# A fused attention and gMLP block: SyncE's transfers in program order during attention, placed by booked engine ends and landing times

## The chip, the cores and the metric

The kernel runs on one core of a Trainium2 chip. The metric is the device time of one execution in microseconds. TensorE (PE in the profile) does the matmuls, VectorE (DVE) and ScalarE (ACT) work on their results, GpSimd (POOL) helps, and SyncE (SP) issues nearly all DMA transfers.

## The reference

The input `x` is 2048 rows of 576. It is normalised, and two branches use the result: a banded attention with 32 heads of width 18, and a gated MLP whose gate mixes the rows with a 2048 x 2048 matrix. Cut to what matters:

```python
xn = layernorm(x)
# A: attention, each row sees itself and the 255 rows before it
q, k, v = split(xn @ wqkv)                      # 32 heads, Dh = 18
p = softmax(where(mask, q @ k.T * Dh**-0.5, -1e9))
s = (p @ v) @ wo
# B: gated MLP, Fh = 2304
z = gelu(xn @ w_in)
z1, z2 = z[..., :Fh], layernorm(z[..., Fh:])
g = w_sp @ z2 + b_sp[:, None]
out = x + s * silu((z1 * g) @ w_out)
```

## The kernel before

Values are kept to float32 by splitting an operand into a high and a low part and multiplying three times (`split`: the high part on ScalarE, the rest on VectorE). The program runs in stages: projections of q, k and v with z2 (up to 447 us), attention with the z1 projection (447 to 987 us), the projection by `wo`, the large product with `w_sp` (`acc`, line 1080), and the last product with `w_out`.

The change lies in the attention stage. It has sixteen **units** of four heads and half of the rows (`UNITS`, eight for the first half, eight for the second). A unit does this:

- Its q and k are loaded from DRAM into **slots** (`att`), five buffers of one pair of heads each, by `load_pair` (lines 343 to 354, sixteen transfers for two pairs). Slots 3 and 4 are cleared first (`clear`).
- **Row maxima** for the softmax are computed one unit ahead (`row_max`): 32 matmuls into `sp` (line 392, two PSUM buffers), a masked maximum on VectorE each (line 396), a transpose (line 402), two operations that make `mhl`, a store to `m_d` (line 410) and four reloads into rows of the slot (line 414), so that the maximum is subtracted inside the score matmul.
- **Scores**: matmuls into `tps` (line 513, two PSUM buffers) and an exponential on ScalarE into `pt` (line 517); then `pv` multiplies by the values `vg` into `ops` (line 537), and ScalarE copies the unit's output to `ou` (line 547).
- **Division** (`finish`): the row sums go from `ou` to `den` by DMA (line 586), VectorE takes the reciprocal (line 559), it is stored to `r_d` and read back, repeated over 32 rows, into `rp` (lines 561 and 564), VectorE multiplies in two halves (line 572), and four stores write `o_d` (line 581).

Between these short matmuls the planner puts the **z1** projection as filling: chunks of 14 matmuls of 512 columns (line 443), a copy `z1o` on ScalarE (line 446) and a store (line 448). The weights of a block of four chunks come by one load `z1raw` (line 421) and are split in six pieces (line 452). In the last unit five pieces of `wo` are loaded (line 715) and split too.

The order on TensorE, VectorE, GpSimd and ScalarE is the order in which this code is run: `tc.manual_schedule` covers them from line 724. The planner keeps a `clock` that every matmul moves on by its booked time (`spend`), the booked ends of ScalarE and VectorE (`busy`, `use`), and a list of jobs with a due time (`after`, run by `tick` once the clock has passed it). SyncE is not covered there: the order of its queue comes from the framework's own scheduler. A transfer is issued when the queue reaches it and its semaphores allow; eight semaphores take turns.

`due` spreads a unit's scores evenly over its span, and the row maxima of the next unit from its begin to the share `RM1` of the span; the first `EARLY` maxima of the unit after that begin at the share `RM2`. `WEIGHT` sets how many z1 matmuls each unit gets.

Of the kernel before, what the change touches and what calls it, by code (L numbers as in the profile page):

```python
# [9 lines left out]
F32 = mybir.dt.float32  # L10
# [6 lines left out]
P = 128  # L17
# [22 lines left out]
EARLY = 6  # L40
RM2 = 0.78
RM1 = 0.74
# [5 lines left out]
_SHARE = [18 + 0.4 * (i >= 8) for i in range(16)]  # L48
# [12 lines left out]
def kernel(  # L61
# [153 lines left out]
    with ExitStack() as early:  # L215
# [109 lines left out]
        with ExitStack() as ph:  # L325
# [3 lines left out]
            def clear(i):  # L329
                eng = (dve, pool)[i % 2]  # L330
                eng.memset(f32(slots[i][:, 0:2 * HS]), 0.0)
                eng.memset(f32(slots[i][:, 2 * HS:]), 1.0)
# [10 lines left out]
            def load_pair(p):  # L343
# [4 lines left out]
                for j in (2 * a, 2 * a + 1):  # L348
                    h, b = 4 * g + j, 64 * (j % 2)
                    q, k = f32(q_of(u, j)), f32(k_of(u, j))  # L350
                    sp.dma_start(q[b:b + 36, :], st_d[0, 0:36, h, q0:q0 + HS])
                    sp.dma_start(k[b:b + 18, :kn], st_d[1, 18:36, h, k0:k0 + kn])
                    sp.dma_start(q[b + 36:b + 56, :], st_d[0, 18:38, h, q0:q0 + HS])
                    sp.dma_start(k[b + 18:b + 54, :kn], st_d[1, 0:36, h, k0:k0 + kn])
# [25 lines left out]

            def row_max(u):
# [3 lines left out]
                for j in range(4):  # L385
                    for i in range(8):
                        qb = 8 * half + i
                        w = 384 if qb >= 2 else 256
# [20 lines left out]
                def put_max():  # L409
                    sp.dma_start(m_d[u], f32(m))  # L410
                    rows = m_d[u].rearrange("(n j i) q -> n j (i q)", n=2, j=4)
# [4 lines left out]
                after(500, put_max)  # L416
# [15 lines left out]
            def z1_matmuls():  # L432
                nxt = z1_first.pop()
                for f in range(FH // P):
# [3 lines left out]
                    for c in range(NC):  # L438
# [3 lines left out]
                        for n, (w, r) in enumerate(pl):  # L442
                            pe.matmul(ps, w, r, start=n == 0, stop=n == len(pl) - 1)  # L443
                            if n == len(pl) - 1:
                                zo = zw.tile([P, 512], F32, name="z1o", bufs=3)
                                act.activation(zo, ps, AF.Copy)
                                use("act", 620)
                                sp.dma_start(z1_d[f * P:(f + 1) * P, cs], zo)
                                if c == 0 and f + 1 < FH // P:
                                    nxt = load_z1(f + 1)  # L450
# [101 lines left out]
            def finish(u, ou):  # L552
# [5 lines left out]
                def put_inverse():  # L558
                    dve.reciprocal(den, den)
                    use("dve", 350)  # L560
                    sp.dma_start(r_d[u].rearrange("h (a b) -> (h a) b", b=HS // 32), den)
# [4 lines left out]
                def invert():  # L566
                    put_inverse()
                    get_inverse()
# [6 lines left out]
                def divide():  # L575
# [3 lines left out]
                    for i in range(4):  # L579
                        h = 4 * g + i  # L580
                        sp.dma_start(o_d[h * DH:(h + 1) * DH, cs], ou[32 * i:32 * i + DH, :])

                if u == NU - 1:
                    last.extend([lambda: sp.dma_start(den, ou[DH::32, :]), put_inverse, get_inverse, divide])
                else:
                    after(700, lambda: sp.dma_start(den, ou[DH::32, :]))
# [126 lines left out]
            def load_wo(k):  # L713
                raw = wors[k % 2]
# [509 lines left out]
```

## Time and profile before

| | |
|---|---|
| median of three timed runs | 1970.8 us (1968.49, 1970.8, 1975.66) |
| the profiled execution | 1975.21 us, its span 1973.5 us |
| TensorE's mean granted clock in it | 0.997 |
| matmuls of attention: z1, scores, row maxima (all units), ops | 1008, 576, 512, 1408 |
| a unit, from its first score to the next one's | 31.0 us (first half, 544.9 to 575.9 us), 33.7 us (second half, 770.5 to 804.2 us) |
| DMA in the profile | 375.58 MB, 190 GB/s in the mean |

In a row of the profile stand the line, the engine, the operation and the tiles it writes and reads; idle time ahead of an instruction is given with the instruction that ended it. `PEld` is the load of weights, which overlaps the matmuls. `SPq` is an instruction of SyncE's queue.

### The profile page before, as it was taken

What the parts mean: (1) busy time and instruction counts of PE and PEld (TensorE: products, weight loads), DVE (VectorE), ACT (ScalarE), POOL (GpSimd) and SP (SyncE); (2) the same over time, 40 slices, a digit from 0 to 9 for tenths busy, and PEclk for the clock granted to TensorE, in tenths of its full rate; (3) what the DMA queues carried; (4) which work ended last, traced back from release to release, by engine and by line L of the source; (5) the groups of instructions that cost most, each with busy time, mean ns of one, the idle gap of its engine ahead of it and who ended that gap; (6) DMA issues with size and microseconds to landing.
All of it is one profiled execution on the core that took longest, in us unless ns stands there. A gap on an engine that the chain in (4) does not pass through costs nothing.

```text
span 1973.5 us, 30747 instructions
## 1 busy us (share of the span) xinstructions
PE 1930.6 (98%) x11096; PEld 1650.5 (84%) x11096; DVE 1054.4 (53%) x2296; ACT 897.9 (45%) x1674; POOL 283.9 (14%) x360
## 2 busy tenths in 40 slices
PE   6999999999999999999899999999999999999998
PEld 5889999997777777777698887888888888899998
DVE  6511233266666666656125778656877567663222
ACT  4222322215555556655546675655554534442121
POOL 5000366202322223323200000000000000000000
PEclk9999999999999999999999999999999999999999
DMA  8656799424454656454476777776677555775441
GB/s 244 181 148 171 247 339 344 178 78 137 139 155 137 160 140 159 137 144 125 141 239 224 258 230 238 249 236 205 209 233 247 181 185 177 263 231 159 140 146 57
DMA packets 221368, 375.58 MB, mean 190 GB/s; under 512 B 43296, under 2 KB 118176, under 8 KB 221088
## 3 DMA queue, kind: packets, MB, share of 16 engines
q1 hardware_dynamic: 205856, 349.66, 57.2%
q10 hardware_dynamic: 15360, 23.97, 3.3%
q8 instruction: 87, 1.43, 0.3%
q14 instruction: 65, 0.53, 0.1%
HBM read 260.45 MB, written 112.83 MB: 189 GB/s over the span
## 4 chain that ended last, share of the span: by engine, by line
PE 85%; DMA 6%; DVE 4%; issue 2%; SPq 1%; ACT 1%; POOL 1%; DVEq 0%; ACTq 0%; POOLq 0%
PE acc L1080 31%; PE po L1151 11%; PE mm L443 10%; PE mm L667 8%; PE mm L296 5%; PE sp L392 5%; PE tps L513 4%; PE ops L537 4%; PE wops L845 3%; PE vps L463 3%; DMA att<-st_d 1%; DMA den<-ou 1%; DMA xr<-in_x_dram 1%; DMA a<-in_w_sp_dram 1%; DVE spl L112 0%
## 5 line engine op out<-in xcount | busy, mean ns | idle before, releaser
L1080 PE MATMUL acc<-spl,zh 128*128 128x512 f32 x1008 | 392.8, 390 | 1.4 <-DVE spl L112 1.2
L1080 PE MATMUL acc<-sph,zl 128*128 128x512 f32 x1008 | 392.2, 389 | 0.0
L1080 PE MATMUL acc<-sph,zh 128*128 128x512 f32 x1008 | 392.2, 389 | 0.0
L396 DVE CUSTOM_DVE_ANT_0 junk<-sp,band 128x384 bf16<-128x384 f32 (+1 forms) x512 | 269.1, 537 | 174.0 <-PE sp L392 167.9
L517 ACT ACTIVATE pt<-tps 128x384 f32<-128x384 f32 (+2 forms) x576 | 244.3, 437 | 190.3 <-PE tps L513 180.1
L443 PE MATMUL mm<-b,z1wh 128*128 128x512 f32 x648 | 236.3, 396 | 0.0
L1080 PEld LDWEIGHTS acc<-spl,zh 128*128 128x128 f32 x1008 | 189.2, 188 | 42.7 <-DVE spl L112 3.5
L112 DVE TENSOR_TENSOR spl<-spr,sph 128x1024 fp32r<-128x1024 f32 x168 | 205.2, 1221 | 32.7 <-ACT sph L111 30.2
L1080 PEld LDWEIGHTS acc<-sph,zh 128*128 128x128 f32 x1008 | 189.2, 188 | 39.2
L1080 PEld LDWEIGHTS acc<-sph,zl 128*128 128x128 f32 x1008 | 189.2, 188 | 39.1
L667 PE MATMUL mm<-z2wh,b 128*128 128x384 f32 x720 | 191.5, 335 | 2.1 <-ACT zt L677 2.1
L111 ACT ACTIVATE zh<-b 128x384 fp32r<-128x384 f32 x168 | 87.4, 521 | 226.9 <-PE acc L1080 226.5
L513 PE MATMUL tps<-att 128*128 128x384 f32 (+1 forms) x576 | 181.5, 325 | 8.2 <-ACT pt L517 8.1
L392 PE MATMUL sp<-att 128*128 128x384 f32 (+1 forms) x512 | 178.1, 354 | 6.5 <-DVE mx L396 3.7
L111 ACT ACTIVATE sph<-spr 128x1024 fp32r<-128x1024 f32 x168 | 175.9, 1047 | 3.3 <-DMA spr<-in_w_sp_dram 3.1
L112 DVE TENSOR_TENSOR zl<-b,zh 128x384 fp32r<-128x384 f32 x168 | 92.9, 553 | 148.0 <-ACT zh L111 142.8
L1151 PE MATMUL po<-b,yh 128*128 128x288 f32 x840 | 145.5, 295 | 0.0
L392 PEld LDWEIGHTS sp<-att 128*128 128x128 f32 x512 | 95.0, 188 | 59.1 <-issue 25.2
L678 DVE BATCH_NORM_STATS2 st<-zt 128x6 f32<-128x384 f32 x96 | 53.4, 559 | 166.8 <-ACT zt L677 166.8
L443 PE MATMUL mm<-b,z1wl 128*128 128x512 f32 x360 | 142.5, 396 | 0.0
L513 PEld LDWEIGHTS tps<-att 128*128 128x128 f32 x576 | 108.2, 189 | 31.3 <-ACT pt L517 15.2
L667 PE MATMUL mm<-z2wl,b 128*128 128x384 f32 x400 | 133.7, 334 | 0.0
(176 smaller groups left out, 2889.2 us busy)
## 6 DMA issues: line engine op xcount, KB each, us to landing
spr<-sc_d SPq DMA_DIRECT2D x96, 512.0 KB
spr<-in_w_sp_dram SPq DMA_DIRECT2D x72, 512.0 KB
zr<-z_d SPq DMA_DIRECT2D x144, 192.0 KB
st_d<-qkhl SPq DMA_DIRECT2D x72, 256.0 KB
z_d<-zt ACTq DMA_DIRECT2D x48, 384.0 KB
z_d<-z1o SPq DMA_DIRECT2D x72, 256.0 KB
z1t<-z_d SPq DMA_DIRECT2D x72, 256.0 KB
y_d<-z1t SPq DMA_DIRECT2D x72, 256.0 KB
```

The costliest lines, as they stand in the source:

```text
L111: act.activation(hi, src, AF.Copy)
L112: dve.tensor_tensor(lo, src, f32(hi), ALU.subtract)
L296: pe.matmul(ps, w, r, start=n == 0, stop=n == len(pl) - 1)
L392: pe.matmul(ps[:, :w], q_of(u, j)[:, i * P:(i + 1) * P], k_of(u, j)[:, k0:k0 + w], start=True, stop=True)
L396: dve.tensor_tensor_reduce(out=junk[:, :w], in0=ps[:, :w], in1=band[:, m0:m0 + w], scale=1.0, scalar=-3.0e38, op0=ALU.add, op1=ALU.max, ac ...
L443: pe.matmul(ps, w, r, start=n == 0, stop=n == len(pl) - 1)
L513: pe.matmul(ps[:, :m * P], k_of(u, j)[:, (kb - base) * P:(kb - base + 1) * P], q_of(u, j)[:, (a - lo) * P:(a - lo + m) * P], start=True, s ...
L517: act.activation(pt[:, j, d0:d0 + n * P], ps[:, (qa - a) * P:(qa - a + n) * P], AF.Exp, scale=scale)
L537: pe.matmul(o_ps[c][32 * j:32 * j + 32, (lo - 4 * c) * P:(hi - 4 * c + 1) * P], vgs[u][:, kb - k0, j * VW:j * VW + 32], pt[:, j, (lo - kb) ...
L667: pe.matmul(ps[:, :ZW], r, wt, start=n == 0, stop=n == len(pl) - 1)
L1080: pe.matmul(acc[j], z[:, ps], w[:, cs], start=s == i == 0 and n in OPENS, stop=s == 7 and i == 2, skip_group_check=True)
L1151: pe.matmul(po[i][:, a, :288], y if ahead else y[:, i * P:(i + 1) * P], w[a], start=f == 0 and m == 0, stop=f == NF - 1 and m == 2)
```

## The change

- SyncE joins the manual order within attention, so its queue holds the transfers in the order in which the code reaches them.
- The sixteen slot loads of a unit become single jobs, due 0.45 us apart from 0.3 us behind the unit's begin.
- The store of `mhl` is placed 0.4 us behind VectorE's booked end, its four reloads 2.6 us later; whatever is left is issued at the unit's end.
- The store of `z1o` is placed 0.2 us behind ScalarE's booked end. `z1raw` is loaded with a block's first matmul, not with the end of its first chunk.
- The load of `den` is placed 0.3 us behind ScalarE's booked end. The reciprocal comes 8 us behind the unit's finish (10 before), `rp` is read 4.8 us later, and the two halves of the division stand at 27.5 and 30 us (22.5 and 24.5 before; 23 and 25 in the last units), which is in the following unit. The stores of `o_d` are 0.4 us apart behind it.
- Both late slots are cleared on GpSimd. ScalarE and VectorE are booked until 4.6 and 4.2 us behind attention's begin, and unit 0 starts its scores and maxima 4 us later, with a larger share of the z1 matmuls.
- Maxima: the first 16 of a unit by the share 0.30 of its span, the rest to 0.765; seven, not six, of the unit after, from 0.81.
- The pieces of `wo` use three buffers, and each split comes five scores later.

```diff
-EARLY = 6
-RM2 = 0.78
-RM1 = 0.74
+EARLY = 7
+RM2 = 0.81
+RM1 = 0.765
+RMH = 0.30
-_SHARE = [18 + 0.4 * (i >= 8) for i in range(16)]
+_SHARE = [18 + 0.4 * (i >= 8) + 6 * (i == 0) for i in range(16)]
...
+                        sp.dma_start(dst, rows)
+                        loaded[p] = loaded.get(p, 0) + 1
+                        yield
...
-                after(500, put_max)
+                to_move[u] = [put_max, get_max]
+                wait = max(busy["dve"] - clock, 0) + 400
+                for ns in (wait, wait + 2600):
+                    after(ns, lambda: to_move[u] and to_move[u].pop(0)())
...
-                                use("act", 620)
-                                sp.dma_start(z1_d[f * P:(f + 1) * P, cs], zo)
-                                if c == 0 and f + 1 < FH // P:
-                                    nxt = load_z1(f + 1)
+                                after(use("act", 620) - clock + 200,
+                                      partial(sp.dma_start, z1_d[f * P:(f + 1) * P, cs], zo))
+                            if n == c == 0 and f + 1 < FH // P:
+                                nxt = load_z1(f + 1)
...
-                    use("dve", 350)
-                    sp.dma_start(r_d[u].rearrange("h (a b) -> (h a) b", b=HS // 32), den)
+                    t = use("dve", 350) - clock + 300
+                    after(t if u < NU - 1 else 0,
+                          lambda: sp.dma_start(r_d[u].rearrange("h (a b) -> (h a) b", b=HS // 32), den))
...
-                    put_inverse()
-                    get_inverse()
+                    after(put_inverse() + 4800, get_inverse)
...
+                            after(busy["dve"] - clock + 200 + 400 * i, partial(store, i))
...
-                    after(700, lambda: sp.dma_start(den, ou[DH::32, :]))
-                    after(10000, invert)
-                    after(22500, partial(divide_half, 0))
-                    after(24500, divide)
+                    after(busy["act"] - clock + 300, lambda: sp.dma_start(den, ou[DH::32, :]))
+                    after(8000, invert)
+                    after(27500 if u < NU - 3 else 23000, partial(divide_half, 0))
+                    after(30000 if u < NU - 3 else 25000, divide)
...
-                raw = wors[k % 2]
+                raw = wors[k % 3]
...
-                clear(i)
+                clear(i, pool)
...
-                heads.enter_context(tc.manual_schedule(engines=ENGINES | {ET.Activation}))
+                heads.enter_context(tc.manual_schedule(engines=ENGINES | {ET.Activation, ET.SP}))
...
-                busy.update(act=clock, dve=clock)
+                busy.update(act=clock + 4600, dve=clock + 4200)
...
-                    for p in (2 * u + 3, 2 * u + 4):
-                        if p < 2 * NU:
-                            load_pair(p)
+                    jobs = [(lambda it=it: next(it, None)) for p in (2 * u + 3, 2 * u + 4) if p < 2 * NU
+                            for it in [pair_jobs(p)] for _ in range(8)]
+                    for i, job in enumerate(jobs):
+                        after(300 + 450 * i + (4000 if u == 0 else 0), job)
...
+                    half_at, end_at = (RMH, RM1) if begun else (0.42, 0.84)
+                    when = [half_at * (n - begun + 0.25) / (16 - begun) if n < 16 else
+                            half_at + 0.01 + (end_at - half_at - 0.01) * (n - 16) / (RMN - 16) for n in range(begun, RMN)]
...
-                        if u == NU - 1 and n % 5 == 1 and 2 <= n // 5 < 7:
+                        if u == NU - 1 and n % 5 == 1 and 3 <= n // 5 < 8:
                             wo_splits.pop(0)()
...
+                    while to_move.get(u + 1):
+                        to_move[u + 1].pop(0)()
```

Where instructions stand now. First TensorE at the begin of attention (`mm` is z1, `sp` a row maximum, `tps` a score). Before, from its first matmul:

```order
L443 MATMUL mm<-b_93,z1wh 128x512
L392 MATMUL sp<-att_1207 128x256
L443 MATMUL mm<-b_95,z1wh 128x512
L513 MATMUL tps<-att_1205 128x384
L443 MATMUL mm<-b_93,z1wl 128x512
```

With the change, from the sixteenth matmul:

```order
L462 MATMUL mm<-b_95,z1wh 128x512
L462 MATMUL mm<-b_93,z1wl 128x512
L462 MATMUL mm<-b_93,z1wh 128x512
L462 MATMUL mm<-b_96,z1wh 128x512
L406 MATMUL sp<-att_1207 128x256
L462 MATMUL mm<-b_93,z1wl 128x512
L532 MATMUL tps<-att_1205 128x384
```

Nineteen z1 matmuls stand ahead of the first row maximum and twenty ahead of the first score, where it was one and two. Then VectorE at the begin of attention, behind the last operation for z2 (`nmr`); `att` is a slot, `junk` and `mx` are a row maximum. Before:

```order
L698 TENSOR_SCALAR nmr_87<-nmr_87 128x16
L331 MEMSET att_4045 128x2048
L332 MEMSET att_4045 128x1280
L396 ISA junk,mx<-sp,band 128x384
L396 ISA mx 128x1
```

With the change:

```order
L122 TENSOR_TENSOR rstd_86<-rstd_86,tm_4022 128x16
L726 TENSOR_TENSOR nmr_87<-mv_85,rstd_86 128x16
L727 TENSOR_SCALAR nmr_87<-nmr_87 128x16
L410 ISA junk,mx<-sp,band 128x256
L410 ISA mx 128x1
```

The clear has left VectorE, and no row maximum of unit 1 stands ahead of `nmr` any more. On ScalarE the first `z1o` copy has moved ahead of the table load for the exponentials.

Then SyncE's queue behind the row maxima that are made in unit 11. The numbered `att` tiles are slots. Before, up to `vg`, with twelve of the sixteen slot loads left out above:

```order
L351 DMA att_4042<-st_d 36x1024
L352 DMA att_4042<-st_d 18x1280
L353 DMA att_4042<-st_d 20x1024
L354 DMA att_4042<-st_d 36x1280
L586 DMA den<-ou 128x1x32
L448 DMA z_d<-z1o 128x512
L421 DMA z1raw<-in_w_z_dram 128x640
L492 DMA vg<-v_d 128x10x89
```

With the change, from the store of the maxima:

```order
L424 DMA m_d<-mhl 64x128
L440 DMA z1raw<-in_w_z_dram 128x640
L385 DMA z_d<-z1o 128x512
L430 DMA att_4040<-m_d 2x1024 x2
L430 DMA att_1205<-m_d 2x1024 x2
L359 DMA att_1207<-st_d 36x1024
L359 DMA att_1207<-st_d 18x1280
```

`z1raw` has moved from behind all slot loads to ahead of them and of the reloads. A `z1o` store stands between the store of the maxima and their reloads here. The row sums of the unit's division come later, as they do one unit on:

```order
L604 DMA o_d<-ou 18x1024
L359 DMA att_4040<-st_d 36x1280
L359 DMA att_1205<-st_d 36x1024
L359 DMA att_1205<-st_d 18x1280
L359 DMA att_1205<-st_d 20x1024
L615 DMA den<-ou 128x1x32
L359 DMA att_1205<-st_d 36x1280
```

`den` now stands behind eleven slot loads and the four `o_d` stores (the last is the first row), where it stood behind sixteen loads.

Last, ScalarE at the end of unit 15, from the first half of its output `oul`; `att_1207` takes the high parts of `wo`. Before:

```order
L547 ACTIVATE oul<-ops 128x512
L517 ACTIVATE pt<-tps 128x384 x2
L446 ACTIVATE z1o<-mm 128x512
L517 ACTIVATE pt<-tps 128x384 x2
L111 ACTIVATE att_1207<-wor 128x576
L517 ACTIVATE pt<-tps 128x256 x4
L517 ACTIVATE pt<-tps 128x128 x4
L446 ACTIVATE z1o<-mm 128x512 x3
```

With the change:

```order
L566 ACTIVATE oul<-ops 128x512
L536 ACTIVATE pt<-tps 128x384 x2
L465 ACTIVATE z1o<-mm 128x512
L536 ACTIVATE pt<-tps 128x384 x2
L112 ACTIVATE att_1207<-wor 128x576
L536 ACTIVATE pt<-tps 128x256 x4
L536 ACTIVATE pt<-tps 128x128
L112 ACTIVATE att_1207<-ou 128x576
L536 ACTIVATE pt<-tps 128x128 x3
L465 ACTIVATE z1o<-mm 128x512 x3
```

The fifth split of `wo` now stands among the last four exponentials.

More of the change, by code (lines that the diff above doesn't have):

```diff
@@ L327, with clear @@
             scale = DH ** -0.5
-            def clear(i):
-                eng = (dve, pool)[i % 2]
+            def clear(i, eng=None):
+                eng = eng or (dve, pool)[i % 2]
                 eng.memset(f32(slots[i][:, 0:2 * HS]), 0.0)
@@ L341, in k_of, with pair_jobs @@
                 return slots[(2 * u + j // 2) % NSLOT][:, 2 * HS:]
-            def load_pair(p):
+            loaded = {}
+            def pair_jobs(p):
                 u, a = divmod(p, 2)
@@ L350, in load_pair @@
                     q, k = f32(q_of(u, j)), f32(k_of(u, j))
[L351 to L354, printed above, removed]
+                    for dst, rows in ((q[b:b + 36, :], st_d[0, 0:36, h, q0:q0 + HS]),
+                                      (k[b:b + 18, :kn], st_d[1, 18:36, h, k0:k0 + kn]),
+                                      (q[b + 36:b + 56, :], st_d[0, 18:38, h, q0:q0 + HS]),
+                                      (k[b + 18:b + 54, :kn], st_d[1, 0:36, h, k0:k0 + kn])):
+                        sp.dma_start(dst, rows)
+                        loaded[p] = loaded.get(p, 0) + 1
+                        yield
+            def load_pair(p):
+                for _ in pair_jobs(p):
+                    pass
             waiting = []
@@ L379, in spend @@
                 tick()
+            to_move = {}
             def row_max(u):
@@ L387, in row_max @@
                         qb = 8 * half + i
+                        assert loaded[2 * u + j // 2] == 8
                         w = 384 if qb >= 2 else 256
@@ L578, in divide, with store @@
                     divide_half(1)
-                    for i in range(4):
+                    def store(i):
                         h = 4 * g + i
                         sp.dma_start(o_d[h * DH:(h + 1) * DH, cs], ou[32 * i:32 * i + DH, :])
+                    for i in range(4):
+                        if u == NU - 1:
+                            store(i)
+                        else:
+                            after(busy["dve"] - clock + 200 + 400 * i, partial(store, i))
                 if u == NU - 1:
@@ L728 @@
                 load_v(0)
-                spend(3000)
+                while to_move[0]:
+                    to_move[0].pop(0)()
                 todo = []
@@ L755 @@
                             + (nmax + nearly) * 185)
-                    t0 = clock
+                    late = 4000 if u == 0 else 0
+                    t0, span = clock + late, span - late
+                    half_at, end_at = (RMH, RM1) if begun else (0.42, 0.84)
+                    when = [half_at * (n - begun + 0.25) / (16 - begun) if n < 16 else
+                            half_at + 0.01 + (end_at - half_at - 0.01) * (n - 16) / (RMN - 16) for n in range(begun, RMN)]
                     due = [[(t0 + span * (n + 0.5) / len(items), 0, n) for n in range(len(items))],
-                           [(t0 + span * (RM1 if begun else 0.84) * (n + 0.25) / nmax, 1, u + 1) for n in range(nmax)]
+                           [(t0 + span * f, 1, u + 1) for f in when[:nmax]]
                            + [(t0 + span * (RM2 + (1 - RM2) * n / nearly), 1, u + 2) for n in range(nearly)]]
@@ L793 @@
                                         ap_.tile([P, HS], F32, name="ou", bufs=2)[:, :D]]
+                            if n == 11:
+                                wors.append(ap_.tile([P, 10, 89], F32, name="vg").rearrange("p a b -> p (a b)")[:, :D])
+                            if n == 1:
                                 wow = [slots[i].rearrange("p c -> p c")[:, :5 * D].rearrange("p (k d) -> p k d", k=5)
@@ L808 @@
                     spend(MM)
-                clock += 100000
-                tick()
+                while waiting:
+                    clock += 100000
+                    tick()
             order.enter_context(tc.manual_schedule(engines=ENGINES | {ET.Activation, ET.SP}))
```

4 lines of the change are left out of this document (added).

## The prediction

> **What bounds the kernel now.** I read the page first, then the waits of TensorE, then those waits one by one in the order of time, and last the queue of SyncE and the order of the two programs.
>
> ```profile
> span 1973.5 us, 30747 instructions
> PE 1930.6 (98%) x11096; PEld 1650.5 (84%) x11096; DVE 1054.4 (53%) x2296; ACT 897.9 (45%) x1674; POOL 283.9 (14%) x360
> ```
>
> TensorE is busy for 1930.6 of 1973.5 us, and the change adds and removes no matmul. So it can only win back idle TensorE time, and only in the stage whose order it changes: the attention units, from 447 us to 987 us. These are all waits of TensorE there (the window runs from 430 us to 1000 us; the columns are total us, number of waits, longest):
>
> ```profile
> PE tps L513 <- ACT pt L517: 8.1, 4, 3.3
> PE sp L392 <- DVE mx L396: 3.7, 5, 1.3
> PE wops L845 <- ACT ohl L831: 2.0, 1, 2.0
> PE sp L392 <- DMA att<-st_d: 1.6, 2, 1.1
> PE sp L392 <- DMA vg<-v_d: 1.0, 1, 1.0
> ```
>
> That is 16.4 us. The wait at L845 stays, because on ScalarE the last three z1o copies, the oul copy and the ohl split follow each other in both programs; 14.4 us are left in 12 waits. Some waits cost more than their length, as the granted clock (after the busy times) shows:
>
> ```profile
> core 0: us, PE busy (x) PEld busy (x) DVE busy (x) ACT busy (x) POOL busy (x), PEclk, DMA share, GB/s
> 850.00:860.00 10.00, 7.71 (x39) 5.27 (x37) 3.29 (x14) 3.50 (x9) 2.44 (x4) 0.83 0.47 144
> 960.00:985.00 25.00, 21.46 (x135) 14.07 (x134) 3.48 (x5) 10.93 (x27) 5.38 (x8) 0.93 0.52 163
> ```
>
> The clock is 0.83 over the 10 us around a wait of 2.3 us at 851 us: 10 x 0.17 = 1.7 us. Around the wait at 968 us it is 0.93 over 25 us: 25 x 0.07 = 1.75 us. [...]
>
> **The change, part by part. Start of attention.**
>
> ```profile
> 448.74 0.40 PE L443 MATMUL mm<-b,z1wl 128*128 128x512 f32 x1
> 449.15 0.63 PE L443 MATMUL mm<-b,z1wh 128*128 128x512 f32 x2
> 452.10 0.44 PE L513 MATMUL tps<-att 128*128 128x384 f32 x1 [2.33 <-ACT pt L517]
> 455.30 0.44 PE L392 MATMUL sp<-att 128*128 128x384 f32 x1 [1.29 <-DVE mx L396]
> 849.38 0.60 ACT L446 ACTIVATE z1o<-mm 128x512 f32<-128x512 f32 x1
> 450.27 1.28 ACT L517 ACT_TABLE_LOAD   x1 [0.56 <-DMA z_d<-zt]
> 451.72 1.76 DVE L331 MEMSET att<- 128x2048 f32 x1 [0.37 <-issue]
> 453.70 1.12 DVE L332 MEMSET att<- 128x1280 f32 x1 [0.21 <-issue]
> 448.84 1.16 POOL L332 MEMSET att<- 128x1280 f32 x1
> ```
>
> The third score cannot start because ScalarE loads a table until 451.55 us, and the row maxima stop while VectorE clears a slot for 2.9 us. The change puts 19 z1 matmuls first. Two of them take 0.63 us where one takes 0.40, so each adds 0.23, and 19 cover 4.4 us, to 451.4 us. The table load now stands behind the first z1o copy, which starts after 14 matmuls, 447.0 + 3.2 + 0.2 = 450.4 us, and takes 0.60 us (the row at 849.38, a later copy of the same size): it ends at 451.0 + 1.28 = 452.3 us. The scores have two PSUM buffers, and the third score follows the first by some 2 us of other matmuls, so it comes after the first exponential. The clear goes to GpSimd, whose own clear ends at 450.0 us; another 2.9 us (estimated from VectorE's) ends near 453 us, no later than VectorE's does now (454.8). Gain: 2.33 + 1.29, and a refill of the pipeline per wait: the second matmul of the x2 row started at 449.38, so 452.10 - 449.38 - 0.23 = 2.49 us were lost where 2.33 are shown, 0.16 more. Together 3.9 us; without that cover they stay.
>
> **z1raw.**
>
> ```profile
> 848.25 0.38 SPq L421 DMA_DIRECT2D z1raw<-in_w_z_dram  x1
> 853.22 0.42 ACT L452 ACTIVATE z1wh<-z1raw 128x256 fp32r<-128x256 f32 x1 [2.86 <-DMA z1raw<-in_w_z_dram]
> 854.07 0.69 PE L513 MATMUL tps<-att 128*128 128x384 f32 x1 [2.29 <-ACT pt L517]
> ```
>
> The weight load stood behind sixteen slot loads and den; ScalarE waited 2.86 us for it and the exponentials behind it kept TensorE. The load is now issued 13 z1 matmuls earlier and, in this unit, ahead of the row maxima's reload and all slot loads. In the next unit those loads went out from 874.32 to 884.81 us (rows below), some 10 us against the 2.86 missing. Gain 2.29 + 0.16 + 1.7 of clock = 4.2 us.
>
> **Splits of wo.**
>
> ```profile
> 962.31 0.57 SPq L564 DMA_DIRECT2D rp<-r_d  x1
> 962.97 0.42 SPq L715 DMA_DIRECT2D wor<-in_wo_dram  x1
> 971.24 0.68 ACT L111 ACTIVATE att<-wor 128x576 fp32r<-128x576 f32 x1 [3.64 <-DMA wor<-in_wo_dram]
> 972.24 0.39 PE L513 MATMUL tps<-att 128*128 128x256 f32 x1 [3.30 <-ACT pt L517]
> ```
>
> The last wo load went out behind the 512 KB of rp and took 8 us. With three buffers all five loads stand ahead of rp, and each split falls five scores later. Gain 3.30 + 0.16 + 1.75 = 5.2 us; against it the last split, 0.68 us on ScalarE, now stands among the last four exponentials, where nothing else fills TensorE. I take all of that off: 4.5 us.
>
> **Reciprocals.**
>
> ```profile
> 874.32 0.29 SPq L351 DMA_DIRECT2D att<-st_d  x1
> 879.06 0.27 SPq L353 DMA_DIRECT2D att<-st_d  x1
> 872.03 2.19 SPq L581 DMA_DIRECT2D o_d<-ou  x4
> 884.81 0.58 SPq L586 DMA_DIRECT2D den<-ou  x1
> 890.77 0.35 DVE L559 RECIPROCAL den<-den 128x32 f32<-128x32 f32 x1 [1.91 <-DMA den<-ou]
> 891.60 0.45 PE L392 MATMUL sp<-att 128*128 128x384 f32 x1 [1.07 <-DVE mx L396]
> 784.69 0.35 DVE L559 RECIPROCAL den<-den 128x32 f32<-128x32 f32 x1 [0.79 <-DMA den<-ou]
> ```
>
> VectorE stands before the reciprocal until den lands; the row maxima queue behind it, and a wait of 1.91 us costs TensorE 1.07 us, while one of 0.79 us costs it nothing (no wait of TensorE is shown near 784.69). The change issues den behind eleven loads and the four o_d stores instead of sixteen loads: in this unit at 879.06 + 0.3 + 2.2 = 881.5 us instead of 884.8. But it also asks for the reciprocal 2 us sooner, at 888.86 - 2 = 886.9 us. With the landing of 6.0 us seen here den is there at 887.5: VectorE would wait 0.6 us, below what reaches TensorE. At stake are the four waits for mx left, 3.7 - 1.3 + 4 x 0.16 = 3.0 us; I take 2.0 us, and 0 to 3.0 as bounds.
>
> **Slot loads.** The three waits for DMA at L392 are row maxima that reach a slot before it is loaded (1.6 + 1.0 + 3 x 0.16 = 3.1 us). Behind the sixteenth maximum of a unit the new rule starts at 0.31 of the span instead of 0.74 x 10.25 / 27 = 0.28, 0.9 us later, and no o_d store stands ahead of the first four loads. I take 2.0 us of 0 to 3.1.
>
> **What it adds.** The last row maximum moves from 0.74 x 26.25 / 27 = 0.719 of a unit to 0.31 + 0.455 x 16 / 17 = 0.738, 0.6 us later in a unit of 31 us, and the next unit's first score waits for the reloads of these maxima:
>
> ```profile
> 573.17 1.19 SPq L414 DMA_DIRECT2D att<-m_d  x4
> 575.88 0.34 PE L513 MATMUL tps<-att 128*128 128x384 f32 x1
> 573.93 0.69 DVE L572 TENSOR_TENSOR ou<-ou,rp 128x512 f32<-128x512 f32 x1
> 870.27 1.22 SPq L414 DMA_DIRECT2D att<-m_d  x4
> 875.51 0.28 PE L513 MATMUL tps<-att 128*128 128x256 f32 x1
> SPq L564 <- DMA r_d<-den: 28.0, 16, 3.6
> SPq L448 <- ACT z1o L446: 69.1, 22, 7.5
> ```
>
> The last of four reloads was issued by 574.36 us, 1.5 us before the score; a small transfer lands in about 28.0 / 16 = 1.75 us (SyncE's mean wait for r_d), so this boundary has no slack. The other one has 875.51 - 871.49 - 1.75 = 2.3 us. I estimate that three of the fifteen are as tight as the first and charge 3 x 0.6 = 1.8 us (bounds 0 and 15 x 0.6 = 9). For new short waits, which no row prices, I charge one as long as the longest on VectorE today, 1.3 us; the bounds are three such, 4 us, and a gain of 1.9 us, a refill of 0.16 at each of the 12 waits, since the same short matmuls get other neighbours. The division's two halves, 0.69 us each on VectorE (the row at 573.93), move into the next unit, whose first maxima are spread thinner; by the plan rp is asked for 12.8 us behind the unit's finish and the halves stand at 27.5 and 30, so they wait for nothing, and I cost them at nothing beside those maxima.
>
> **Sum.** 3.9 + 4.2 + 4.5 + 2.0 + 2.0 - 1.8 - 1.3 = 13.5 us, from the profiled execution's 1975.2 to 1961.7 us. That execution lies 4.4 us above the median of the three timed runs, 1970.8; the reciprocals and slot loads depend on the landings of one execution, so I count 2.5 of their 4.0 us: 12.0 us off the median, **1958.8 us**.
>
> **Rivals.** (1) Only the three large waits go. The reciprocal, asked for 2 us sooner, waits again wherever den lands over 6 us after its issue, and the tight boundaries take 0.4 us at each of fifteen: 12.6 - 6 - 2.6 (twice the 1.3) = 4 us, 1967 us. For it: the margin of 0.6 us above; against it: den's queue is shorter by five loads. (2) Slower: SyncE now keeps program order, and at seven of the fifteen boundaries a z1o store stands between the m_d store and its reloads. If TensorE runs behind the planner's clock, the store waits for ScalarE with the reloads behind it, and the first score waits for both. Today's slack, 1.0 us in the mean of the two boundaries above, shrinks to 0.4, so it decides where the store is over 0.4 us late. SyncE's waits for z1o are 69.1 / 22 = 3.1 us in the mean and 7.5 at most; at the middle, 5.3, it is 7 x (5.3 - 0.4) = 34 us against 16.6 gained: 1988 us. [...] Against it: the store is now placed by ScalarE's booked end plus 0.2 us. (3) The waits go and come back behind the stage, at the first ohl split or the first acc matmuls: no net change, 1970 us; little speaks for it, since the loads there follow TensorE.
>
> **How the numbers follow.** Forecast 0.57, rival (1) 0.30, (2) 0.08, (3) 0.05. All five terms at their full size with nothing added give 3.9 + 4.2 + 5.2 + 3.0 + 3.1 = 19.4 us, 1951 us; with the gain of 1.9 from neighbours it is 1950. Above, the range takes in rivals (1) and (3): 1971. About 0.5% (9.9 us) is what a measurement of this kernel can tell from no change: faster 0.57, same 0.35, slower 0.08.
>
> **What would show it.** The first 10 us of attention without a wait of TensorE; no ACT wait for z1raw or wor, and the clock 1.00 at 850 and 960 us; waits of the reciprocal for den below 1 us; waits of tps for att<-m_d at the boundaries, none in the trace before, are what I charged 1.8 us. I am wrong if SyncE shows z1o waits ahead of the reloads, or if VectorE waits for den as often as before.

## The result, and the profile after

| | before | with the change |
|---|---|---|
| median of six timed runs each, taken together | 1970.69 us (1968.49 to 1979.27) | 1957.7 us (1956.93 to 1958.83) |
| ratio | | 0.9922, 95% interval 0.9908 to 0.9937 |
| the profiled execution (its span) | 1975.21 us (1973.5) | 1958.83 us (1957.1) |
| TensorE's mean granted clock in it | 0.997 | 0.999 |

The kernel is 13.0 us faster by the medians and 16.4 us by the profiled executions. First the page of the changed kernel, the same two lines as of before:

```profile
span 1957.1 us, 30722 instructions
PE 1925.8 (98%) x11096; PEld 1648.7 (84%) x11096; DVE 1054.3 (54%) x2294; ACT 898.0 (46%) x1674; POOL 283.1 (14%) x362
```

The matmuls are the same 11096, and TensorE still bounds the kernel. Its waits from 430 to 1000 us (total us, number, longest):

```profile
PE wops L886 <- ACT ohl L872: 2.0, 1, 2.0
PE tps L532 <- ACT pt L536: 0.7, 2, 0.4
PE sp L406 <- issue: 0.6, 1, 0.6
PE sp L406 <- DVE mx L410: 0.5, 2, 0.3
PE wops L886 <- DVE ohl L873: 0.3, 1, 0.3
```

The 16.4 us of waits before have become 4.1, and half of that is the wait for `ohl` that neither program avoids. The stretches whose clock the prediction spoke of, by the windows of the changed kernel (PE busy, PEld, DVE, ACT, POOL, then the granted clock):

```profile
447.00:487.00 40.00, 39.67 (x235) 30.73 (x234) 25.79 (x97) 23.06 (x49) 14.42 (x18) 1.00 0.45 130
800.00:900.00 100.00, 99.92 (x689) 75.05 (x689) 62.44 (x216) 60.82 (x148) 29.83 (x48) 1.00 0.55 147
...
970.00:975.00 5.00, 3.27 (x13) 2.93 (x14) 3.44 (x5) 2.64 (x3) 0.00 (x0) 0.68 0.80 257
```

The first 40 us of attention are full, the 100 us that held the wait for `z1raw` are full at full clock, and one loss of clock is left, 5 x 0.32 us here and 5 x 0.02 us in the next window (0.98 to 980 us), 1.7 us together, behind the wait for `ohl`. (It lies in the 25 us that showed 0.93 before, and they show 0.93 again; the wait for `ohl` has moved into them.) The windows of before:

```profile
447.00:487.00 40.00, 36.08 (x230) 27.32 (x229) 27.77 (x101) 22.69 (x49) 11.56 (x16) 1.00 0.42 120
...
853.00:858.00 5.00, 3.94 (x17) 3.00 (x21) 1.13 (x4) 2.97 (x8) 1.22 (x2) 0.66 0.22 68
...
970.00:975.00 5.00, 2.76 (x19) 0.96 (x19) 1.96 (x3) 1.96 (x5) 0.89 (x1) 0.85 0.10 34
975.00:980.00 5.00, 4.79 (x22) 3.79 (x19) 0.00 (x0) 1.54 (x5) 0.63 (x1) 0.81 0.74 219
...
985.00:990.00 5.00, 2.98 (x15) 2.62 (x12) 2.86 (x4) 3.21 (x4) 0.00 (x0) 0.71 0.58 175
990.00:995.00 5.00, 5.00 (x37) 5.00 (x37) 0.65 (x2) 1.25 (x2) 0.00 (x0) 0.95 0.57 158
```

Before had three such losses: 5 x 0.34 = 1.7 us behind `z1raw`, 0.75 + 0.95 = 1.7 behind `wo`, 1.45 + 0.25 = 1.7 behind `ohl`. Two are gone. So the profiled gain of 16.4 us is 12.3 us of waits, 3.4 us of clock, and 0.7 us that neither shows; refills behind the waits may be in it.

What did not change is VectorE's wait ahead of the reciprocals, of before and of the change:

```profile
DVE den L559 <- DMA den<-ou: 6.1, 7, 1.9
```

```profile
DVE den L578 <- DMA den<-ou: 6.0, 8, 1.6
```

### The profile page after: what moved, and what is told of

The parts are those of the page before. It is cut to its first block, busy times and chain, and to the rows that moved or that the text cites. A ratio compares the mean times of both kernels' runs of the same rounds, so it can differ in the third digit from the quotient of the medians.

```text
span 1957.1 us, 30722 instructions
## 1 busy us (share of the span) xinstructions
PE 1925.8 (98%) x11096; PEld 1648.7 (84%) x11096; DVE 1054.3 (54%) x2294; ACT 898.0 (46%) x1674; POOL 283.1 (14%) x362
## 4 chain that ended last, share of the span: by engine, by line
PE 91%; DMA 4%; DVE 4%; issue 1%; ACT 1%; SPq 0%; DVEq 0%; ACTq 0%
PE acc L1121 31%; PE mm L462 11%; PE po L1192 11%; PE mm L696 11%; PE mm L297 6%; PE sp L406 5%; PE tps L532 5%; PE ops L556 4%; PE wops L886 3%; PE vps L482 3%; DMA xr<-in_x_dram 1%; DMA a<-in_w_sp_dram 1%; DMA sc_d<-a 1%; DMA zr<-z_d 0%; DVE spl L113 0%
## 5 line engine op out<-in xcount | busy, mean ns | idle before, releaser
L462 PE MATMUL mm<-b,z1wh 128*128 128x512 f32 x648 | 230.3, 395 | 0.0
L696 PEld LDWEIGHTS mm<-z2wh,b 128*128 128x128 f32 x720 | 130.4, 188 | 4.6 <-ACT zt L706 4.6
```

Of the source, the lines that this page charges most:

```text
L696: pe.matmul(ps[:, :ZW], r, wt, start=n == 0, stop=n == len(pl) - 1)
```

## The experiments

All twelve leave the computation as it is. Times are medians of several runs of each kernel; the changed kernel stands at 1957.7 us. The kernel before, run beside each group, gave 1973.7, 1974.4 and 1972.7 us, so small differences are read from the medians of the variants, whose runs lie closer together, and from their waits. The changed kernel itself was not run again beside these groups: a difference of 1 or 2 us to its 1957.7 us, with no wait in the trace to go with it, is not shown to be real.

### Parts taken back one at a time

**The start of attention** (`u_start`):

```diff
-_SHARE = [18 + 0.4 * (i >= 8) + 6 * (i == 0) for i in range(16)]
+_SHARE = [18 + 0.4 * (i >= 8) for i in range(16)]
...
-                clear(i, pool)
+                clear(i)
...
-                busy.update(act=clock + 4600, dve=clock + 4200)
+                busy.update(act=clock, dve=clock)
...
-                        after(300 + 450 * i + (4000 if u == 0 else 0), job)
+                        after(300 + 450 * i, job)
...
-                    late = 4000 if u == 0 else 0
+                    late = 0
```

> The changed kernel with the begin of attention as it was: no extra 4 us of z1 matmuls, no booked ends, no larger share for unit 0, and slot 4 cleared on VectorE again. Theory (each large wait went by its own edit): two waits of TensorE return near 450 us, about 2.3 us for an exponential and 1.3 us for a row maximum, with their refills 3.9 us in all: 1957.7 + 3.9 = 1961.6 us. Rival (the waits went because SyncE's queue is in another order): no wait there, 1957.7 us within 1 us.

Measured: 1966.42 us, ratio to before 0.9965 (0.9949 to 0.9981), 8.7 us slower than the changed kernel. TensorE's waits:

```profile
PE tps L532 <- ACT pt L536: 3.3, 4, 2.3
PE sp L406 <- DVE mx L410: 2.8, 2, 2.6
```

and the windows around them:

```profile
450.00:455.00 5.00, 1.31 (x5) 0.57 (x4) 3.37 (x10) 3.44 (x6) 1.10 (x1) 1.00 0.57 154
455.00:460.00 5.00, 3.81 (x10) 3.32 (x11) 2.75 (x9) 0.49 (x1) 0.92 (x2) 0.54 0.74 173
460.00:465.00 5.00, 5.00 (x21) 4.36 (x21) 2.56 (x10) 2.45 (x5) 0.55 (x2) 0.77 0.47 146
```

The same two waits are back, 2.3 us for the table load and 2.6 (before: 1.29) for the maxima, about 4.9 us of idle time, and here the clock falls too: 2.3 + 1.15 = 3.45 us, twice 1.7. Together that is 8.3 of the 8.7 us. In the trace before the same spot kept its clock (1.00 from 447 to 487 us). The edits at the start do what the prediction said; what they are worth depends on whether the clock falls behind the waits.

**The load of z1raw** (`u_z1raw`) and **the pieces of wo** (`u_wo`):

```diff
-                            if n == c == 0 and f + 1 < FH // P:
-                                nxt = load_z1(f + 1)
+                                if c == 0 and f + 1 < FH // P:
+                                    nxt = load_z1(f + 1)
```

> The changed kernel with z1raw loaded again with the end of a block's first chunk, 13 z1 matmuls later. Theory (the early load took the wait at 851 us away): ScalarE waits over 2 us for z1raw in at least one unit, TensorE over 1.5 us behind it, the granted clock of those 10 us falls below 0.9: 1957.7 + 4.2 = 1961.9 us. Rival (the new places of the slot loads and of den keep SyncE's queue short, so that the load is in time at its old place too): no wait for z1raw, 1957.7 us within 1 us.

```diff
-                raw = wors[k % 3]
+                raw = wors[k % 2]
...
-                        if u == NU - 1 and n % 5 == 1 and 3 <= n // 5 < 8:
+                        if u == NU - 1 and n % 5 == 1 and 2 <= n // 5 < 7:
...
-                            if n == 11:
-                                wors.append(ap_.tile([P, 10, 89], F32, name="vg").rearrange("p a b -> p (a b)")[:, :D])
```

> The changed kernel with two buffers for the pieces of wo and the splits five scores sooner, as before. Theory (buffers and later splits took the wait at 968 us away): ScalarE waits about 3 us for the last piece and TensorE behind it, 1957.7 + 4.5 = 1962.2 us. Rival (program order alone puts the loads ahead of rp): waits below 0.5 us, 1957.7 us within 1 us.

Measured: 1959.1 us (7 runs) and 1958.01 us (5 runs), 1.4 and 0.3 us slower, where the prediction had put 4.2 and 4.5 on them. With `z1raw` at its old place ScalarE waits twice, shortly:

```profile
ACT z1wh L471 <- DMA z1raw<-in_w_z_dram: 2.4, 2, 1.6
...
PE tps L532 <- ACT pt L536: 1.4, 3, 0.8
```

With two buffers for `wo` no wait for them is left at all. So the two large waits of before do not hang on these two edits alone.

**Both together** (`u_z1wo`), since either could cover for the other:

> The changed kernel with z1raw at its old place and the pieces of wo on two buffers with the earlier splits, both at once; alone they cost 1.4 and 0.3 us. Theory (the two are independent and both nearly covered by the queue's new order): 1957.7 + 1.7 = 1959.4 us. Rival (each covers for the other): the waits of the kernel before return, 1957.7 + 8.7 = 1966.4 us.

Measured: 1958.54 us, 0.8 us slower; one wait for `z1raw` of 1.6 us, none for `wo`. They do not cover for each other.

**The reciprocal** (`u_rec10`):

```diff
-                    after(8000, invert)
+                    after(10000, invert)
```

> The changed kernel with the reciprocal 10 us behind a unit's finish instead of 8 (rp follows it, 2 us later too). In the changed kernel VectorE stands 6.0 us before sixteen reciprocals until den lands, as long as before the change (6.1 us). Theory A (this wait still reaches TensorE in two units, 0.59 and 0.30 us): VectorE's wait for den falls below 1 us and the time by 0.9 us with the refills, to 1956.8 us. Theory B (the row maxima are thin there now, so the wait costs nothing, and what TensorE waits has another cause): 1957.7 us within 0.5 us, and TensorE's waits of that size stay. Rival (rp is 2 us later and the divisions wait for it): VectorE waits over 1 us for rp and the time rises by 0.5 us or more.

Measured: 1957.58 us, no change. VectorE no longer waits for any `den` of units 0 to 14 (6.0 us in the changed kernel). TensorE's waits hardly gain from it:

```profile
PE tps L532 <- DMA att<-m_d: 0.9, 1, 0.9
...
PE sp L406 <- DVE mx L410: 0.2, 1, 0.2
```

There are 0.3 us less behind the maxima and 0.9 us more behind a reload at a unit's boundary. The 0.6 us of "issue" are gone too, but in the changed kernel they stand at 678.36 us, ahead of the nearest wait for `den` (680.18 to 681.82), and cannot come from it. So the trace puts at most 0.3 us of TensorE's time on 6.0 us of this wait; that the two times are equal is also the doing of the new wait for a reload.

**The rule of the row maxima** (`u_rmold`), one even slope to 0.765 of the span:

```diff
-                    half_at, end_at = (RMH, RM1) if begun else (0.42, 0.84)
-                    when = [half_at * (n - begun + 0.25) / (16 - begun) if n < 16 else
-                            half_at + 0.01 + (end_at - half_at - 0.01) * (n - 16) / (RMN - 16) for n in range(begun, RMN)]
+                    when = [(RM1 if begun else 0.84) * (n - begun + 0.25) / (RMN - begun) for n in range(begun, RMN)]
```

> The changed kernel with the row maxima of a unit on one slope to the share 0.765, as before the change (there to 0.74), so that more of them stand around the reciprocal. Theory (VectorE still waits 6 us for den; TensorE is spared because the maxima are thin there): TensorE's waits for mx rise from 0.5 to 2 us or more, the time by 1.5 to 3 us, to 1959.2 to 1960.7. Rival (the slope makes no difference): 1957.7 us within 0.7 us.

Measured: 1960.87 us, 3.2 us slower by the medians. (The ratio to the kernel before hides it, 0.9925 against 0.9922, since that kernel ran at 1974.4 us beside this one.) The waits say where:

```profile
PE sp L406 <- DMA att<-st_d: 2.9, 4, 1.2
```

It is the slots that are not loaded yet, not the reciprocals (0.2 us for `mx` are left): with one slope the maxima behind the sixteenth reach a slot too early. 2.9 us and four refills of 0.16 are 3.5.

**The place of the division** (`divold`):

```diff
-                    after(27500 if u < NU - 3 else 23000, partial(divide_half, 0))
-                    after(30000 if u < NU - 3 else 25000, divide)
+                    after(22500, partial(divide_half, 0))
+                    after(24500, divide)
```

> The changed kernel with the division's halves at 22.5 and 24.5 us behind the unit's finish, as before the change, in place of 27.5 and 30 (23 and 25 in the last units). Theory A (the division has slack on VectorE wherever it stands): 1957 to 1958.5, no wait longer than in the changed kernel. Theory B (the halves, 0.69 us each, then stand among the last maxima of the unit or rp has not landed): VectorE waits for rp or the reloads of the maxima come later, tps waits for att<-m_d or sp for mx sum to 3 us or more, 1961 to 1964.

Measured: 1967.32 us (1961.67 to 1970.78, 10 runs), ratio 0.9971 (0.996 to 0.9983): 9.6 us slower, the dearest part of all. TensorE's waits, and VectorE's for the data of the division:

```profile
DVE ou L594 <- DMA rp<-r_d: 7.8, 4, 2.7
...
PE sp L406 <- DVE mx L410: 6.2, 9, 2.0
...
PE sp L406 <- DMA att<-st_d: 3.2, 4, 1.4
```

The timeline shows the usual case, on VectorE and on TensorE, at the end of a unit:

```profile
511.74 0.69 DVE L594 TENSOR_TENSOR ou<-ou,rp 128x512 f32<-128x512 f32 x1
512.35 0.55 DVE L410 CUSTOM_DVE_ANT_0 junk<-sp,band 128x384 bf16<-128x384 f32 x1
...
512.04 0.34 PE L406 MATMUL sp<-att 128*128 128x384 f32 x1
...
512.96 0.45 PE L406 MATMUL sp<-att 128*128 128x384 f32 x1 [0.47 <-DVE mx L410]
```

The early maxima of the unit after now follow each other every 0.6 us at the end of a unit, and a half of 0.69 us does not fit between two of them. TensorE waits 0.47 us at 512.96, and the same at 545.17, 576.41, 607.44, 638.65 and 669.87 us, six times in all. In the second half of the rows it is `rp` that has not landed:

```profile
801.53 0.69 DVE L594 TENSOR_TENSOR ou<-ou,rp 128x512 f32<-128x512 f32 x1 [2.62 <-DMA rp<-r_d]
...
802.75 0.44 PE L406 MATMUL sp<-att 128*128 128x384 f32 x1 [1.97 <-DVE mx L410]
```

and the windows around it:

```profile
800.00:805.00 5.00, 3.03 (x17) 1.48 (x19) 2.93 (x9) 1.64 (x4) 1.00 (x3) 0.85 0.13 41
805.00:810.00 5.00, 5.00 (x29) 3.17 (x22) 2.50 (x9) 1.21 (x5) 0.94 (x2) 0.81 0.77 220
```

That wait takes 1.97 us and 0.75 + 0.95 = 1.7 us of clock. The slots are late, for 3.2 us, because the `o_d` stores come with the division: around 670 us they now stand among the first slot loads, and SyncE issues a block of twelve loads from 671.97 us, where in the changed kernel a block of thirteen goes out from 668.46 us; the maximum at 681.37 us then waits 1.42 us for its slot. (The other three such waits were not followed up.) In the changed kernel the halves stand among the first maxima of the following unit, where VectorE has time between them: behind the two halves at 516.72 and 519.11 us it waits 0.18, 0.61 and 0.34 us for the next maxima.

**SyncE's program order** (`u_nosp`), all placements kept:

```diff
-                heads.enter_context(tc.manual_schedule(engines=ENGINES | {ET.Activation, ET.SP}))
+                heads.enter_context(tc.manual_schedule(engines=ENGINES | {ET.Activation}))
```

> The changed kernel with SyncE's queue left to the framework's scheduler, every other edit kept. Theory P (the program order carries the gain behind the begin of attention): waits of TensorE of over 1 us return behind 500 us, 8 us in all, 1966 us. Theory Q (the places of work on the engines, the early z1raw and the third buffer carry it): 1957.7 us within 2 us; SyncE's queue differs, but what it loads is in time.

Measured: 1957.07 us (1955.17 to 1958.88): no difference. The order by itself is worth nothing once the transfers are placed.

### Three parts taken back together

`nosp3` takes back SyncE's order, the place of `z1raw` and the buffers of `wo` (the three diffs above).

> The changed kernel with three parts undone together: SyncE out of the manual order within attention, z1raw loaded at the end of a block's first chunk, wo with two buffers and splits five scores earlier. What stays of SyncE's side: the booked due times of den, rp, z1o, m_d and slot loads. Theory A (those due times and the new filling keep z1raw and wo in time): 1958 to 1959.5, ScalarE's waits for z1raw and wor below 2 us each. Theory B (any one of the three parts is enough, but one is needed): the waits of 2.9 and 3.6 us are back with clock below 0.95 around them, 1964 to 1967.

Measured: 1961.63 us (1959.65 to 1963.88), ratio 0.9942 (0.9923 to 0.9961), 3.9 us slower. One of the two waits is back:

```profile
ACT att L112 <- DMA wor<-in_wo_dram: 4.1, 1, 4.1
PE tps L532 <- ACT pt L536: 4.0, 2, 3.7
```

with its loss of clock in the windows:

```profile
955.00:960.00 5.00, 1.27 (x5) 0.71 (x3) 1.31 (x3) 1.61 (x4) 0.27 (x1) 0.89 0.14 53
960.00:965.00 5.00, 4.69 (x27) 2.23 (x27) 0.65 (x2) 1.79 (x6) 1.20 (x2) 0.77 0.31 71
```

So for `wo` either the program order (`u_wo`) or the buffers and later splits (`u_nosp`) are enough, and without both it costs 3.9 us, `z1raw` at its old place included (the pair was not taken back alone). For `z1raw` none of the three is needed: the shortest time from a load's issue to its first use is 6.8 us here (740.37 to 747.15 us), with no wait, against 10.3 us in the changed kernel (446.2 to 456.5) and 4.97 us, 2.86 of them waited for, at 848.25 us before. What keeps it in time here was not isolated by a run; left are the due times of the transfers around it and the places to which the blocks have moved. The traces speak for the due times: in `b_start` (below) the blocks stand at nearly the same times, and the load for the one that splits at 816 us goes out at 811.37 us, behind sixteen slot loads and `den`; in `nosp3` the load for the one at 811 us goes out at 792.68 us, ahead of the reloads and all slot loads of that unit.

### Parts put into the kernel before, alone

**Only SyncE's program order** (`u_sponly`, the line of `u_nosp` the other way round, in the kernel before):

> The kernel before with one edit: SyncE in program order within attention, every transfer left where the code issued it. Theory P (the program order takes the waits for z1raw and wo away): ScalarE's waits for z1raw and wo, 2.9 and 3.6 us before, fall below 1 us, and the time falls by about 8 us, to 1963 us, where before is 1971. Theory Q (the places do it; here rp is read straight behind r_d's store, ahead of the last piece of wo, as before): ScalarE still waits 2 us or more for the last piece, and the time stays within 3 us of before.

Measured: 2010.56 us (2007.77 to 2016.1), ratio 1.0182 (1.015 to 1.0214), some 36 us slower:

```profile
ACT z1wh L452 <- DMA z1raw<-in_w_z_dram: 30.3, 6, 9.4
PE tps L513 <- ACT pt L517: 25.4, 6, 7.1
```

and in SyncE's queue:

```profile
SPq L448 <- ACT z1o L446: 105.3, 24, 10.8
```

One of the six, on SyncE, ScalarE and TensorE:

```profile
565.90 0.35 SPq L448 DMA_DIRECT2D z_d<-z1o  x1
566.43 0.36 SPq L421 DMA_DIRECT2D z1raw<-in_w_z_dram  x1
...
572.29 0.42 ACT L452 ACTIVATE z1wh<-z1raw 128x256 fp32r<-128x256 f32 x1 [9.36 <-DMA z1raw<-in_w_z_dram]
...
573.14 0.69 PE L513 MATMUL tps<-att 128*128 128x384 f32 x1 [7.05 <-ACT pt L517]
```

The weight load stands behind a `z1o` store and that behind sixteen slot loads, which go out one by one from 555.86 to 564.44 us; ScalarE stands 9.36 us for it, the exponentials queue behind ScalarE, and TensorE stands 7.05 us. In this run SyncE waits ahead of `z1o` stores for 105.3 us, 10.8 at most (the row above), and ahead of the slot loads of line 351 for other slot loads 24 times, 17.5 us in all and 1.2 at most. With such waits in SyncE's queue this kernel takes some 36 us longer.

**Only the start** (`b_start`, the reverse of the diff of `u_start`, in the kernel before):

> The kernel before, with only the start of attention changed: larger share of z1 matmuls for unit 0, both late slots cleared on GpSimd, ScalarE and VectorE booked 4.6 and 4.2 us ahead, unit 0's scores and maxima 4 us later. SyncE's order, the loads, the row maxima's slope, den and division stay. Theory A (the trace of before prices the start): 3.9 us less than before, ratio 0.998; the waits of 2.3 and 1.3 us in the first 10 us gone, ScalarE's waits for z1raw (2.9) and wor (3.6) still there. Theory B (the price that undoing the start in the changed kernel gave, 8.7 us): ratio 0.9955, about 1962. Theory C (the z1raw and wo waits hang on where the z1 matmuls fall, not on SyncE): both are gone or halved already here, and the ratio is below 0.9945.

Measured: 1969.72 us (1967.34 to 1974.75), ratio 0.9988 (0.9977 to 1.0): 2 to 3 us, with an interval that ends at no change. The waits of the first 10 us are gone, and the later two have grown:

```profile
PE tps L513 <- ACT pt L517: 7.6, 4, 4.4
...
ACT att L111 <- DMA wor<-in_wo_dram: 4.7, 1, 4.7
...
ACT z1wh L452 <- DMA z1raw<-in_w_z_dram: 3.2, 1, 3.2
```

TensorE's wait for `wo` is 4.4 us where it was 3.3, that for `z1raw` 2.63 (at 817 us) where it was 2.29: 1.5 us of what the start wins are given back there, and by the windows that held it the wait for `wo` costs 3.4 us of clock now (0.51 from 965 to 970 us, 0.81 to 975), where it was 1.7. The waits for `z1raw` and `wo` do not go with the start, so they hang on what the change does to the transfers, or on another of its parts. The 2.4 us that row maxima waited for `mx` behind the start, nearly all of it behind late reciprocals, are gone here, though nothing of the reciprocals was changed.

**The start and the new rule of the maxima** (`b_start_rm`):

> The same with the new rule for the row maxima as well (first sixteen by 0.30 of the span, the rest to 0.765, seven of the unit after from 0.81). Nothing of SyncE is changed. Theory A (each part's price from the trace of before): 3.9 + 2.0, ratio 0.997; waits for z1raw, wor and den as before. Theory B (start and maxima carry the gain, as the runs that undo parts add up: 8.7 + 3.2 = 11.9): ratio 0.994, about 1959, with no ScalarE wait for z1raw or wor above 1.5 us. Theory C (without the placed transfers the new order of maxima runs into loads that are late): same as before or slower, waits of sp for att<-st_d above 3 us.

Measured: 1971.11 us (1968.82 to 1975.8), ratio 0.9991 (0.9981 to 1.0002): the new rule brings nothing here.

```profile
PE sp L393 <- DVE mx L397: 6.4, 10, 1.5
```

Six of the ten are 0.47 us long and stand at the ends of units (512.92, 544.00 and on), as in `divold`: the new rule with the old division makes the collision, in whichever kernel. Two more, 1.49 and 1.44 us, stand behind reciprocals that wait 2.33 and 2.51 us for `den`. What the rule does win is the waits for slots: 1.7 us in `b_start`, none here.

## Why the prediction was right

The forecast of 1958.8 us is 1.1 us from the 1957.7 measured. By its steps:

- **What can be won.** Right: the gain lies in attention, in TensorE's waits and their clock; 12.3 + 3.4 of the 16.4 us by the profile.
- **Start, 3.9.** Right in mechanism and size for the profiled execution: 39.67 - 36.08 = 3.6 us and two refills. What it is worth in the time is less fixed: 8.7 us taken out of the changed kernel, where the clock falls there too, and 2 to 3 us put into the kernel before.
- **z1raw, 4.2, and wo, 4.5.** Right in size: both waits and both losses of clock are gone, and the charge of 0.68 us for the last split shows as two waits of together 0.7 us among the last exponentials (one of them, 0.3 us, stays in `u_wo`, whose splits come earlier). The cause was told too narrowly. The step named one edit for each; `u_z1raw` and `u_wo` put 1.4 and 0.3 us on those edits. For `wo` there are two sufficient causes, the order and the buffers, and `nosp3`, without either, is 3.9 us slower. For `z1raw` none of the three parts tried is needed; the rest of the change is enough, and the traces of `b_start` and `nosp3` point at the due times of the slot loads, which no run isolates.
- **Reciprocals, 2.0.** The size came about: waits for `mx` behind the start were 3.7 - 1.3 = 2.4 us and are 0.5. The mechanism failed. "Waits of the reciprocal for den below 1 us" is wrong: they sum to 6.0 us as before and reach 1.64, since the reciprocal is asked for sooner, as rival (1) had it. Where they are longest they cost nothing, because no maximum stands in that place. Before, TensorE had maxima every 0.8 us around the reciprocal at 717.46, which waits 1.52 us:

```profile
715.82 0.34 PE L392 MATMUL sp<-att 128*128 128x384 f32 x1
...
716.64 0.34 PE L392 MATMUL sp<-att 128*128 128x384 f32 x1
...
718.29 0.44 PE L392 MATMUL sp<-att 128*128 128x384 f32 x1 [0.68 <-DVE mx L396]
```

  With the change, around one that waits 1.64 us, to 681.82:

```profile
679.25 0.34 PE L406 MATMUL sp<-att 128*128 128x384 f32 x1
...
681.58 0.62 PE L406 MATMUL sp<-att 128*128 128x384 f32 x2
```

  For 2.3 us it does other matmuls, and the wait falls into that gap. That an edit of the change made the gap is not shown: in `b_start` a wait of 1.52 us (at 854.18 us) costs TensorE nothing with the old rule of the maxima, and in `b_start_rm` waits of 2.33 and 2.51 us cost it 1.49 and 1.44 with the new one. That the size came about is luck as far as these runs tell.
- **Slot loads, 2.0.** Right: 1.6 + 1.0 us of waits are gone, the rule alone takes 1.7 us of them away from `b_start`, and taking it back (`u_rmold`) brings 2.9. The 0.6 us of "issue" at 678.36 may be a rest of them, since before waited for a slot at 678.65.
- **Charges, 1.8 and 1.3.** Too high. No first score waits for its reloads, so the 1.8 are 0; the new short waits are at most the 0.6 us of "issue". That is 2.5 of the 16.4 - 13.5 = 2.9 us by which the profile was underestimated.
- **The division, "at nothing".** Here a step failed as well. As a term the zero is right, but as a part of the change it is not free to leave out: at its old place it costs 9.6 us. The trace of `divold` shows what that is made of: six collisions, 2.8 us, with the maxima that the new rule packs every 0.6 us at a unit's end, just where the old halves stood; 3.2 us behind `rp`, which the change asks for 12.8 us behind the finish (10 before); 3.2 us of late slots; and 1.7 us of clock. The prediction looked at the new place alone and not at what the other edits do to the old one.
- **The slower rival.** A blocked store can cost that much, some 36 us in `u_sponly`; but what stands behind it there is `z1raw`, not the reloads, so it is chance that the size is close to the rival's 34. In the changed kernel SyncE does hold a `z1o` store between the store of the maxima and their reloads, at three of the boundaries for 0.9 to 1.4 us, the longest at 728.46 us:

```profile
SPq L385 <- ACT pt L536: 1.4, 1, 1.4
```

  (The releaser named is ScalarE's operation next to the `z1o` copy.) Still no score waits for a reload. That the placements by booked ends keep these waits short, as the prediction argued, fits that; `u_sponly` lacks them, but is another kernel in other respects too.
- **The signs named ahead.** No wait of TensorE in the first 10 us, none of ScalarE for `z1raw` or `wor`, and the full clock at 850 us came as foretold; from 960 to 985 us the clock is 0.93 by the wait for `ohl` alone. Both signs of being wrong came too: VectorE waits for `den` as often as before (eight times, it was seven), and SyncE shows `z1o` waits ahead of reloads. Neither reached TensorE by more than 0.3 us. Rival (3), waits that come back behind the stage, is out: the span is shorter by the 16.4 us of the profiled times.
- **From the profile to the median.** Of the 13.5 us the prediction counted 12.0 off the median. The profiled gain was larger than that of the medians by 3.4 us, so the discount of 1.5 had the right sign. That the forecast lies so close is in part luck: the profiled gain was put 2.9 us too low and the discount 1.9 us too low, and the two nearly cancel.

Taken back one by one, the parts add up to 8.7 + 9.6 + 3.2 + 1.4 + 0.3 - 0.1 - 0.6 = 22.5 us, where the whole gives 13.0; put in, the start and the rule give 2. No part has a price of its own: maxima and division go together, order and placement go together, and what one wait returns another may take.

## What to carry to other kernels

Price an edit also at the place it leaves: an instruction of 0.7 us that "costs nothing" where it goes may have to go, because another edit of the same change needs its old place. A wait on a side engine counted here only where TensorE had something queued behind it: VectorE's 6.0 us of waits for `den` were worth at most 0.3 us (`u_rec10`). Before a queue is put in program order, give every transfer in it a place by the end of what it waits for; the order alone lost some 36 us, and with the places it gained nothing by itself, though for `wo` it can stand in for the third buffer.

## What the runs showed of the hardware

In these runs the clock was lost in pieces of one size. The windows above give 1.7 us behind a wait of 2.29 us (`z1raw`, before), of 3.30 (`wo`, before), of 1.97 (`divold`) and of 3.73 (`nosp3`: 0.55 + 1.15), and twice that behind the pair in `u_start` (3.45) and behind 4.42 us in `b_start` (3.4). The length of the wait alone does not set it: in `u_sponly` a wait of 5.01 us is followed by 1.7 us again (0.92 from 915 to 920 us, 0.74 to 925). Behind the pair of 2.33 and 1.29 us at the start of attention, before, nothing was lost, and nothing behind the 2.02 us for `ohl` in `u_wo` (1.00 in every window from 960 to 995 us). How much idle time brings a loss, these runs do not show: a wait of 1.97 us was enough once, and waits of 2.02 and 2.33 us were not.

The spread of the times goes with the clock. In 52 timed runs of the kernel before, beside the experiments, the mean clock lay between 0.994 (six runs, 1978.1 us in the mean) and 0.999, most often at 0.997 (fifteen, 1971.7 us); its mean, 0.9962, is 7.5 us of 1970. Five of the changed kernel's six runs show 0.999, about 2 us. The median of the 52 runs is 1973.2 us, 15.5 above the changed kernel's, and by this estimate some 5.5 of the 15.5 us are clock, more than the 3.4 of the one profiled execution. (The clock is given in steps of 0.001, which are 2 us, so the 5.5 is rough.)
